# Attention and experts on one core: value tiles packed around resident ones, low parts of the keys written in place

## The chip, the cores and the metric

The kernel runs on one core of one Trainium2 chip. The metric is the device time of one execution in microseconds (us), the median of several runs; lower is better.

## The reference

Attention over q, k, v of shape (8, 8, 576, 64), in fp32, with a bias from a running sum of s, followed by a layer of 16 experts of which each token uses one:

```
scores = q @ k^T / 8 + min(-(cum[q] - cum[k]), 0),  cum = cumsum(max(s, 0)); causal
attn   = exp(scores - rowmax);  attn /= sum(attn) + 1e-9
x      = attn @ v                       -> 4608 tokens x 512
expert = argmax of a group, then argmax within it
out    = weight * relu(x @ w1[expert]) @ w2[expert]
```

The change lies in the attention part alone.

## The kernel before, in words

The 64 heads are worked off as 32 pairs p of two heads n = 2p and 2p + 1. For each pair four inputs are brought into SBUF:

- `load_raw` (L143): keys and queries of both heads, transposed, as `r` (128 partitions x 2 x 576; one head in partitions 0 to 63, the other in 64 to 127), from DRAM.
- `split` (L145 to L158): each value is cut into a rounded high part and the remainder, the low part. The high parts are cast by ScalarE (L150) into the tile `hl`, whose four slots are key high, query high, key low, query low. The low parts are a subtraction on GpSimd (L153; VectorE for pair 0): one instruction of 128 x 576 for the keys, one for the queries. `split` issues the cast, and the subtraction goes into a list "G" from which it is taken later.
- `load_a` and `load_b` (L166 to L185): DMAs within SBUF copy from `hl` into two operand tiles. `WA` gets key high and query high (64 partitions). `WB` has 128 partitions: its lower 64 hold key low and query high, its upper 64 key high and query low. For each head the lower half is one DMA (L184, 64 x 2 x 576, 288 KB) and the upper half another (L185, 288 KB). `WB` has three buffers.
- `load_v` (L187): the values, one DMA from DRAM of 480 KB. The tile `VT` holds for each of five key tiles three blocks of 64 columns: values of head 0, ones, values of head 1. The ones lie in DRAM with the values and are loaded each time. `VT` has two buffers.

TensorE then computes, for each head, row maxima (L209, `pm`, read by VectorE at L217), the scores as a product of `WA` (L265) and one of `WB` (L267) into `ps`, and the product with the values (L305, `po`). The stationary operand at L305 is 128 columns wide: values and ones side by side, so that half of `po` is the row's sum. ScalarE takes the exponential (L275) and empties `po` in two steps, `vals` (L309) and `sums` (L312). GpSimd sets what lies above the diagonal to zero (L284, AFFINE_SELECT) before L305 reads it. The shift by the row maximum goes through two small DMAs, `WA<-th` and `WA<-tl` (L243), which ScalarE issues in its own queue.

The order of work on TensorE, VectorE, ScalarE and GpSimd is written out by hand as strings of letters, one string for the step of an even head and one for that of an odd one (`ORDERS`, `FIRST`): B and C are score and value products, A row maxima, `b` an exponential, `e` a causal select, `v` the emptying of `po`, `G` a subtraction from the list, `S` a split. SyncE (SP) issues the loads; after the first steps its order is set by a scheduler from the program's order.

Of the kernel before, what the change touches and what calls it, by code (L numbers as in the profile page):

```python
# [8 lines left out]
F32 = mybir.dt.float32  # L9
# [11 lines left out]
P = 128  # L21
# [26 lines left out]
NB = 5  # L48
# [59 lines left out]
def attention(tc, qk, v, s, wr, xs, st):  # L108
# [3 lines left out]
    with ExitStack() as ctx:  # L112
# [18 lines left out]
        NA, NBB, NVT = 4, 3, 2  # L131
        WA = [wa.tile([68, 2, 2, QW], F32R, name=f"WA{i}") for i in range(NA)]
        WB = [wa.tile([P, 2, 2, S], F32R, name=f"WB{i}") for i in range(NBB)]
        VT = [big.tile([P, NB, 3, 64], F32, name=f"VT{i}", tag=f"VT{i}", bufs=1) for i in range(NVT)]
# [10 lines left out]
        def split(p, part, later=False):  # L145

            if part == 0:
                hls[p] = raw.tile([P, 4, S], F32R, name=f"hl{p}", tag="hl", bufs=3)
            hl, r = hls[p], raws[p]
            nc.scalar.copy(hl[:, part], r[:, part])  # L150

            def low():
                (nc.vector if p < 1 else nc.gpsimd).tensor_tensor(  # L153
                    out=hl[:, 2 + part], in0=r[:, part], in1=hl[:, part].bitcast(F32), op=ALU.subtract)

            if later:
                push("G", p, low)
            else:  # L158
                low()
# [16 lines left out]
        def load_b(p, placed=False):  # L176
            w = WB[p % NBB].bitcast(F32)
            hl = hls.pop(p).bitcast(F32)
            for h in range(2):

                hr = slice(h * 64, h * 64 + 64)
                a = slice(0, 1 if placed and h == 0 else 2)
                b = slice(1 if placed and h else 0, 2)
                nc.sync.dma_start(w[0:64, a, h], hl[hr, 2:0:-1][:, a])  # L184
                nc.sync.dma_start(w[64:128, b, h], hl[hr, 0::3][:, b])  # L185

        def load_v(p):  # L187
            nc.sync.dma_start(VT[p % NVT], v[p])
# [100 lines left out]
        def av(n, pt, vals, sums):  # L289
# [4 lines left out]
            for half, todo in enumerate(avs):  # L294
# [4 lines left out]
                def item(j, t, qa, qb, half=half, base=base, w=w, po=po, last=len(todo) - 1):  # L299
                    if j == 0:  # L300
# [5 lines left out]
                                     VT[p % NVT][:, t, h:h + 2].rearrange("p a d -> p (a d)"),  # L306
# [106 lines left out]
        def push(k, i, f):  # L413
            fifo[k].append((i, f))
# [67 lines left out]
        for i in range(2):  # L482
# [24 lines left out]
        ones(3)  # L507

# [1011 lines left out]
def _layout(inputs):  # L1520
# [7 lines left out]
    vv = np.ones((NP, NB * P, 3, D), dtype=v.dtype)  # L1528
    vp = v.reshape(NP, 2, S, D)
    vv[:, :S, 0], vv[:, :S, 2] = vp[:, 0], vp[:, 1]  # L1530
    vv = vv.reshape(NP, NB, P, 3, D).transpose(0, 2, 1, 3, 4)
# [30 lines left out]
```

## Time and profile before

| | us |
|---|---|
| median of 3 runs (975.96 to 977.0) | 976.94 |
| the profiled execution | 975.5 |
| its span on the core | 973.8 |

The attention takes the first 460 us or so of the span, the experts the rest. In the rows below PE is TensorE's matmul, PEld its weight load, DVE VectorE, ACT ScalarE, POOL GpSimd and SP SyncE; a trailing q (ACTq, SPq) is the engine's own queue of instructions, in which it issues DMAs. A wait is put down to the work that came last by the profile.

### The profile page before, as it was taken

How to read it: one execution, taken by the hardware profiler on the slowest of the kernel's cores; microseconds unless marked ns; L12 is line 12 of the kernel's file. 1: busy time of each engine (PE TensorE's matmuls, PEld its weight loads, DVE VectorE, ACT ScalarE, POOL GpSimd, SP SyncE). 2: the span in 40 equal slices, each digit the busy share in tenths (PEclk: the TensorE clock that was granted, in tenths of full speed). 3: DMA queues.
4: the chain of work that ended last, by engine and by line, in shares of the span. 5: the costliest groups of instructions: out<-in, count | busy, mean ns of one | idle time of the engine just before them, and what ended most of it. 6: DMA issues, size and time to landing. Idle time of an engine off the chain costs nothing. (4 is left out here: it accounts for less than half of the span.)

```text
span 973.8 us, 17866 instructions
## 1 busy us (share of the span) xinstructions
PE 881.4 (91%) x5640; PEld 790.7 (81%) x5640; DVE 747.9 (77%) x2023; ACT 610.5 (63%) x1388; POOL 550.5 (57%) x682
## 2 busy tenths in 40 slices
PE   4888998999999999998868899999999999999983
PEld 3677887887777787886657799999999999998972
DVE  7445686697868779787497679988888998888860
ACT  5556775776767667776535356676766666766640
POOL 8444455453554456443566556667776767766640
PEclk9989998999999999999888899999999999999997
DMA  7999999999999999953624444555655556655410
GB/s 201 244 221 232 244 238 217 238 240 231 233 231 229 234 222 241 228 132 113 200 85 164 172 156 154 194 196 180 216 188 183 193 180 217 217 205 205 153 42 22
DMA packets 64167, 187.25 MB, mean 192 GB/s; under 512 B 9628, under 2 KB 18460, under 8 KB 55872
## 3 DMA queue, kind: packets, MB, share of 16 engines
q1 hardware_dynamic: 54160, 166.11, 62.8%
q0 software_dynamic: 7488, 18.89, 5.5%
q10 hardware_dynamic: 2416, 1.03, 0.5%
q8 instruction: 47, 0.77, 0.3%
q14 instruction: 56, 0.46, 0.2%
HBM read 112.12 MB, written 19.69 MB: 135 GB/s over the span
## 5 line engine op out<-in xcount | busy, mean ns | idle before, releaser
L971 POOL TENSOR_TENSOR wl<-raw,wh 128x512 fp32r<-128x512 f32 x166 | 214.4, 1305 | 76.1 <-ACT wh L968 58.2
L217 DVE CUSTOM_DVE_ANT_0 mx<-pm,mask 128x192 bf16<-128x192 f32 (+4 forms) x320 | 127.7, 419 | 63.4 <-PE pm L209 61.0
L968 ACT CAST wh<-raw 128x512 fp32r<-128x512 f32 x256 | 155.1, 616 | 9.6 <-issue 9.5
L1069 PE MATMUL ph<-xl,wh 128*128 128x256 f32 (+13 forms) x512 | 146.3, 305 | 4.3 <-DVE xl L1041 4.0
L1069 PE MATMUL ph<-xh,wh 128*128 128x256 f32 (+13 forms) x512 | 145.3, 302 | 4.1 <-ACT xh L1040 4.0
L209 PE MATMUL pm<-WA 66*128 66x288 f32 (+4 forms) x384 | 126.2, 360 | 20.0 <-DMA WA<-ch 10.6
L265 PE MATMUL ps<-WA 68*128 68x320 f32 (+4 forms) x384 | 137.1, 361 | 5.8 <-ACT pu L275 2.7
L305 PE MATMUL po<-pt,VT 128*128 128x256 f32 (+3 forms) x512 | 124.5, 361 | 17.0 <-DMA VT<-in_v_dram 7.5
L284 POOL TENSOR_SCALAR_AFFINE_SELECT pt<-pt 128x128 f32<-128x128 f32 (+2 forms) x192 | 63.9, 340 | 104.9 <-ACT pt L275 102.4
L305 PEld LDWEIGHTS po<-pt,VT 128*128 128x128 f32 x512 | 88.7, 195 | 33.6 <-issue 14.2
L1124 PE MATMUL py<-hl,wh 128*128 128x256 f32 (+13 forms) x448 | 113.9, 302 | 1.7 <-DVE hl L1065 1.7
L1124 PE MATMUL py<-hh,wh 128*128 128x256 f32 (+13 forms) x448 | 113.6, 302 | 0.7 <-ACT wh L968 0.6
L267 PE MATMUL ps<-WB 128*128 128x320 f32 (+4 forms) x384 | 112.3, 305 | 0.0
L1036 DVE STREAM_TRANSPOSE xt<-xg 32x256 f32<-32x256 f32 (+1 forms) x224 | 109.5, 489 | 3.4
L1170 DVE STREAM_TRANSPOSE yr<-yT 32x384 f32<-32x384 f32 (+1 forms) x208 | 104.5, 502 | 4.3
L305 PE MATMUL po<-pu,VT 128*128 128x320 f32 (+1 forms) x384 | 106.9, 387 | 0.0
L1069 PEld LDWEIGHTS ph<-xl,wh 128*128 128x128 f32 x512 | 97.5, 190 | 7.9 <-DVE xl L1041 6.1
L1069 PEld LDWEIGHTS ph<-xh,wh 128*128 128x128 f32 x512 | 97.6, 191 | 6.1 <-ACT xh L1040 5.9
L209 PEld LDWEIGHTS pm<-WA 66*128 66x128 f32 (+1 forms) x384 | 70.3, 195 | 31.8 <-DVE mc L217 12.2
L367 POOL TENSOR_TENSOR xTl<-xT,xTh 128x512 fp32r<-128x512 f32 x30 | 38.2, 1274 | 101.8 <-ACT xTh L363 90.5
L1064 ACT ACTIVATE hh<-ph 128x256 fp32r<-128x256 f32 (+13 forms) x128 | 53.8, 420 | 62.0 <-PE ph L1069 60.9
L153 POOL TENSOR_TENSOR hl<-r,hl 128x576 fp32r<-128x576 f32 x62 | 88.0, 1422 | 4.2 <-ACT hl L150 4.2
(238 smaller groups left out, 2014.2 us busy)
## 6 DMA issues: line engine op xcount, KB each, us to landing
raw<-in_w_dram SPq DMA_DIRECT2D x64, 1024.0 KB
WB<-hl SPq DMA_DIRECT2D x122, 288.0 KB
r<-in_qk_dram SPq DMA_DIRECT2D x32, 576.0 KB
WA<-hl SPq DMA_DIRECT2D x61, 288.0 KB
VT<-in_v_dram SPq DMA_DIRECT2D x32, 480.0 KB
xs<-xr SPq DMA_DIRECT2D x15, 512.0 KB
WA<-cumd SPq DMA_DIRECT2D x56, 4.5 KB
xs<-xrt SPq DMA_DIRECT2D x7, 128.0 KB
```

The lines of the kernel that those rows point to most:

```text
L153: (nc.vector if p < 1 else nc.gpsimd).tensor_tensor(out=hl[:, 2 + part], in0=r[:, part], in1=hl[:, part].bitcast(F32), op=ALU.subtract)
L209: nc.tensor.matmul(ps[:rows, :cw], WA[i][0:66, QA, h, QO + q0:QO + q0 + rows], WA[i][0:66, KA, h, QO + c0:QO + c0 + cw], start=True, stop= ...
L217: nc.vector.tensor_tensor_reduce(out=tmp[:rows, :cw], in0=ps[:rows, :cw], in1=mk[:rows], scale=1.0, scalar=-3.0e38 if c0 == 0 else mo, op0 ...
L265: nc.tensor.matmul(ps[:rows, o:o + w], WA[i][0:68, KA, h, QO + k0:QO + k0 + rows], WA[i][0:68, QA, h, QO + q0:QO + q0 + w], start=True, st ...
L267: nc.tensor.matmul(ps[:rows, o:o + w], WB[p % NBB][:, KA, h, k0:k0 + rows], WB[p % NBB][:, QA, h, q0:q0 + w], start=False, stop=True)
L305: nc.tensor.matmul(po[0][:, qa - base:qb - base], VT[p % NVT][:, t, h:h + 2].rearrange("p a d -> p (a d)"), x[:, c:c + qb - qa], start=(j ...
L968: self.casts.append(nc.scalar.copy(h[:, j], raw[:, j]))
L971: self.low = nc.gpsimd.tensor_tensor(out=l[:, j], in0=raw[:, j], in1=h[:, j].bitcast(F32), op=ALU.subtract)
L1036: V.transpose(dst[:, 0:n, :, j], src[:, 0:n, :, i])
L1069: self.product = nc.tensor.matmul(pss[f][:, :cap], w[f // 4][:, c, (f % 4) * P:(f % 4 + 1) * P], x[:, c, :cap], start=(c == 0 and w is sel ...
L1124: self.product = nc.tensor.matmul(pss[c][:, :cap], w[2 + f // 4][:, f % 4, c * P:(c + 1) * P], x[:, f, :cap], start=(f == 0 and w is self. ...
L1170: V.transpose(dst[:, 0:n, :, i], src[:, 0:n, :, j])
```

## The change

`VT` holds per block the values of head 1 of the tile before, the values of head 0 of this tile, and ones, so that the two blocks of values lie side by side; the ones are set once, at the start, by two GpSimd MEMSETs, and the load writes only the values, in six pieces of 512 bytes per partition instead of one of 3840. The 128 columns that L305 uses are the same ones. GpSimd (VectorE for pair 0) writes the low parts of the keys straight into the lower half of `WB`, in one instruction of 64 x 576 per head, so `hl` has three slots instead of four and the DMA of the lower half of `WB` carries only the query's high part. `WB` has five buffers instead of three. The order strings get one more `G` per pair.

```diff
-        NA, NBB, NVT = 4, 3, 2
+        NA, NBB, NVT = 4, 5, 2
-        VT = [big.tile([P, NB, 3, 64], F32, name=f"VT{i}", tag=f"VT{i}", bufs=1) for i in range(NVT)]
+        VT = [big.tile([P, NB + 1, 3, 64], F32, name=f"VT{i}", tag=f"VT{i}", bufs=1) for i in range(NVT)]
...
-                hls[p] = raw.tile([P, 4, S], F32R, name=f"hl{p}", tag="hl", bufs=3)
+                hls[p] = raw.tile([P, 3, S], F32R, name=f"hl{p}", tag="hl", bufs=3)
...
-            def low():
+            def low(h):
+                hr = slice(0, P) if part else slice(h * 64, h * 64 + 64)
                 (nc.vector if p < 1 else nc.gpsimd).tensor_tensor(
-                    out=hl[:, 2 + part], in0=r[:, part], in1=hl[:, part].bitcast(F32), op=ALU.subtract)
-
-            if later:
-                push("G", p, low)
-            else:
-                low()
+                    out=hl[:, 2] if part else WB[p % NBB][0:64, KA, h], in0=r[hr, part],
+                    in1=hl[hr, part].bitcast(F32), op=ALU.subtract)
+
+            for h in range(1 if part else 2):
+                if later:
+                    push("G", p, lambda h=h: low(h))
+                else:
+                    low(h)
...
-                a = slice(0, 1 if placed and h == 0 else 2)
                 b = slice(1 if placed and h else 0, 2)
-                nc.sync.dma_start(w[0:64, a, h], hl[hr, 2:0:-1][:, a])
-                nc.sync.dma_start(w[64:128, b, h], hl[hr, 0::3][:, b])
+                if h or not placed:
+                    nc.sync.dma_start(w[0:64, QA, h], hl[hr, 1])
+                nc.sync.dma_start(w[64:128, b, h], hl[hr, 0::2][:, b])
...
-            nc.sync.dma_start(VT[p % NVT], v[p])
+            nc.sync.dma_start(VT[p % NVT][:, :, 0:2], v[p])
...
-                                     VT[p % NVT][:, t, h:h + 2].rearrange("p a d -> p (a d)"),
+                                     VT[p % NVT].rearrange("p t a d -> p (t a d)")[:, (3 * t + 1 + h) * 64:][:, 0:P],
...
+        for t in VT:
+            nc.gpsimd.memset(t[:, 0:NB, 2], 1.0)
...
-            "b S R B0 R v b a A0 B2 v C0 e G a R a B3 T C1 A3 B1 A2 C2 b e t C3 v C4 B4 J b D v e a a A1 "
+            "b S R B0 R v b a A0 B2 v C0 e G a R a B3 T C1 A3 B1 A2 C2 b e t C3 v G C4 B4 J b D v e a a A1 "
```

How the order moves. First GpSimd, around one pair in the middle of the attention; `hl`, `r`, `pt`, `pu`, `xTl` are the tiles named above, with numbers of their buffers. Before:

```order
L367 TENSOR_TENSOR xTl_768<-xT_1239,xTh_767 128x512
L284 AFFINE_SELECT pu_118<-pu_118 128x128
L284 AFFINE_SELECT pt_117<-pt_117 128x128
L153 TENSOR_TENSOR hl_1168<-r_996,hl_1168 128x576
L284 AFFINE_SELECT pt_117<-pt_117 128x2x128
L284 AFFINE_SELECT pt_117<-pt_117 64x64
L284 AFFINE_SELECT pt_115<-pt_115 128x128
L153 TENSOR_TENSOR hl_1348<-r_1165,hl_1348 128x576
L284 AFFINE_SELECT pu_116<-pu_116 128x128
L284 AFFINE_SELECT pt_115<-pt_115 128x2x128
L284 AFFINE_SELECT pt_115<-pt_115 64x64
```

and now:

```order
L371 TENSOR_TENSOR xTl_776<-xT_1250,xTh_775 128x512
L288 AFFINE_SELECT pu_120<-pu_120 128x128
L288 AFFINE_SELECT pt_119<-pt_119 128x128
L155 TENSOR_TENSOR hl_1178<-r_1005,hl_1178 128x576
L288 AFFINE_SELECT pt_119<-pt_119 128x2x128
L288 AFFINE_SELECT pt_119<-pt_119 64x64
L288 AFFINE_SELECT pt_117<-pt_117 128x128
L155 TENSOR_TENSOR WB_110<-r_1175,hl_1359 64x576
L288 AFFINE_SELECT pu_118<-pu_118 128x128
L155 TENSOR_TENSOR WB_110<-r_1175,hl_1359 64x576
L288 AFFINE_SELECT pt_117<-pt_117 128x2x128
L288 AFFINE_SELECT pt_117<-pt_117 64x64
```

The one subtraction for the keys has become two, and the second stands ahead of the last two selects of the even head's step. Next the DMAs of SP for about one pair, with what each waits for (DMAHW0 to DMAHW7 are eight semaphores that the DMAs of SP and ScalarE take in turn: a DMA that waits for DMAHW5 is issued when the last one on DMAHW5 has landed, and then uses it itself). Before:

```order
L172 DMA WA_109<-hl_2323 64x2x576 [waits DMAHW4_49,Activation_49]
L188 DMA VT_113<-in_v_dram 128x960 [waits DMAHW5_49,PE_49]
L402 DMA xs<-xr_2252 128x4x256 [waits DMAHW6_49,Activation_49]
L172 DMA WA_109<-hl_2323 64x2x576 [waits DMAHW7_49,PE_49]
L174 DMA WA_109<-cumd 2x576 [waits DMAHW0_49]
L184 DMA WB_112<-hl_2117 64x2x576 [waits DMAHW1_49,PE_49]
L185 DMA WB_112<-hl_2117 64x2x576 [waits DMAHW2_49]
L143 DMA r_2509<-in_qk_dram 128x1152 [waits DMAHW3_49,Pool_49]
L174 DMA WA_106<-cumd 2x576 [waits DMAHW6_49,PE_49]
```

and now:

```order
L192 DMA VT_115<-in_v_dram 128x6x128 [waits DMAHW3_49,PE_49]
L176 DMA WA_109<-hl_2339 64x2x576 [waits DMAHW4_49,Activation_49]
L188 DMA WB_110<-hl_2339 64x576 [waits DMAHW5_49]
L188 DMA WB_110<-hl_2339 64x576 [waits DMAHW6_49]
L406 DMA xs<-xr_2268 128x4x256 [waits DMAHW7_49,Activation_49]
L176 DMA WA_109<-hl_2339 64x2x576 [waits DMAHW0_49,PE_49]
L178 DMA WA_109<-cumd 2x576 [waits DMAHW1_49]
L144 DMA r_2526<-in_qk_dram 128x1152 [waits DMAHW2_49,Pool_49]
L189 DMA WB_110<-hl_2339 64x2x576 [waits DMAHW3_49]
L189 DMA WB_110<-hl_2339 64x2x576 [waits DMAHW4_49]
L178 DMA WA_106<-cumd 2x576 [waits DMAHW7_49,PE_49]
```

The value load now stands ahead of the loads of `WA` and `WB`, and the loads of `WB` no longer wait for TensorE. The gap in the numbers before the last row is ScalarE's two small DMAs, which stand in its queue ahead of `sums`. Before:

```order
L309 COPY vals_2413<-po_0_2540 64x256 [waits PE_49]
L275 ACTIVATE pt_115<-ps_2_0_2555 128x512 [waits Pool_49]
L243 DMA WA_107<-th_2574 1x10x128 [waits DMAHW4_49,DVE_49]
L243 DMA WA_107<-tl_2575 1x10x128 [waits DMAHW5_49,DVE_49]
L312 ACTIVATE sums_2414<-po_0_2540 64x256
```

and now:

```order
L313 COPY vals_2430<-po_0_2557 64x256 [waits PE_49]
L279 ACTIVATE pt_117<-ps_2_0_2572 128x512 [waits Pool_49]
L247 DMA WA_107<-th_2591 1x10x128 [waits DMAHW5_49,DVE_49]
L247 DMA WA_107<-tl_2592 1x10x128 [waits DMAHW6_49,DVE_49]
L316 ACTIVATE sums_2431<-po_0_2557 64x256
```

Read with SP's rows: before, they are issued when a load of `WA` (on DMAHW4) and one of `VT` (on DMAHW5) have landed; now, when two loads of `WB` of half the former size have (on DMAHW5 and DMAHW6).

## Rows read from the trace of the kernel before

**Rows 1.** The page: busy time of each engine, and DMA busy tenths in 40 slices.
```profile
PE 881.4 (91%) x5640; PEld 790.7 (81%) x5640; DVE 747.9 (77%) x2023; ACT 610.5 (63%) x1388; POOL 550.5 (57%) x682
DMA  7999999999999999953624444555655556655410
```

**Rows 2.** Busy time by stage; the last three columns: granted clock, DMA share, GB/s.
```profile
25.00:56.00 31.00, 26.28 (x120) 22.16 (x120) 11.96 (x50) 15.41 (x36) 12.66 (x21) 0.89 1.04 240
56.00:167.82 111.82, 101.11 (x596) 86.30 (x595) 73.10 (x272) 77.28 (x192) 54.71 (x93) 0.94 1.01 230
167.82:400.63 232.81, 219.86 (x1389) 182.50 (x1388) 183.95 (x654) 163.09 (x410) 120.67 (x200) 1.00 1.00 233
400.00:425.00 25.00, 24.97 (x164) 22.11 (x163) 21.11 (x83) 18.14 (x46) 12.68 (x24) 1.00 0.88 213
```

**Rows 3.** What TensorE waits for, 60 to 430 us: total, times, longest.
```profile
PE po L305 <- DMA VT<-in_v_dram: 7.5, 5, 2.5
PE pm L209 <- DVE mc L217: 5.7, 7, 1.9
PE po L305 <- DMA WA<-tl: 4.3, 4, 1.4
PE po L305 <- ACT sums L312: 2.3, 1, 2.3
PE ps L265 <- DMA WA<-tl: 0.8, 2, 0.7
```

**Rows 4.** One such wait: TensorE's row at 278.56 us.
```profile
278.56 0.67 PE L305 MATMUL po<-pt,VT 128*128 128x256 f32 x2 [1.33 <-DMA WA<-tl]
```

**Rows 5.** ScalarE's rows just before it: start, duration, in brackets idle before.
```profile
275.75 0.72 ACTq L243 DMA_DIRECT2D WA<-th  x1
277.29 0.75 ACTq L243 DMA_DIRECT2D WA<-tl  x1
278.08 0.38 ACT L312 ACTIVATE sums<-po 64x256 f32<-64x256 f32 x1 [2.29 <-DVE mc L217]
```

**Rows 6.** DMA issues of the page: count, and size of one.
```profile
WB<-hl SPq DMA_DIRECT2D x122, 288.0 KB
VT<-in_v_dram SPq DMA_DIRECT2D x32, 480.0 KB
WB<-hl SPq DMA_DIRECT2D x6, 144.0 KB
```

**Rows 7.** Stretches with a lower granted clock (columns as in rows 2).
```profile
48.00:53.00 5.00, 4.68 (x17) 4.27 (x18) 1.46 (x8) 2.43 (x7) 2.55 (x5) 0.50 1.04 226
92.00:96.00 4.00, 4.00 (x22) 3.84 (x20) 2.27 (x10) 3.66 (x10) 2.62 (x4) 0.66 1.00 207
156.00:160.00 4.00, 2.36 (x7) 2.08 (x8) 0.50 (x5) 1.36 (x4) 0.23 (x1) 0.52 0.94 190
160.00:164.00 4.00, 4.00 (x20) 3.84 (x20) 2.26 (x8) 3.46 (x9) 2.58 (x4) 0.63 0.92 199
```

**Rows 8.** DMA queues of the page: packets, MB, share of 16 engines over the span.
```profile
q1 hardware_dynamic: 54160, 166.11, 62.8%
q10 hardware_dynamic: 2416, 1.03, 0.5%
```

**Rows 9.** L153: duration in ns (least, median, most), first and last start.
```profile
L153 POOL TENSOR_TENSOR hl<-r,hl x62: 1397/1408/1972, 11.8 to 409.2; 128x576 fp32r<-128x576 f32 x62
```

**Rows 10.** ScalarE, 167 to 401 us: the same columns on 128 and on 64 partitions.
```profile
L275 ACT ACTIVATE pt<-ps 128x256 f32<-128x256 f32 x34 | 13.0, 382 | 0.1
L312 ACT ACTIVATE sums<-po 64x256 f32<-64x256 f32 x34 | 12.8, 378 | 34.5 <-DVE mc L217 20.9 <-DVE xT L350 8.7 <-DVE st L342 4.7
```

**Rows 11.** GpSimd in an even step, then TensorE's reader of that block.
```profile
262.55 0.28 POOL L284 TENSOR_SCALAR_AFFINE_SELECT pu<-pu 128x128 f32<-128x128 f32 x1
262.80 0.40 POOL L284 TENSOR_SCALAR_AFFINE_SELECT pt<-pt 128x256 f32<-128x256 f32 x1
268.35 0.70 PE L305 MATMUL po<-pt,VT 128*128 128x320 f32 x2
```

**Rows 12.** GpSimd at the start: a MEMSET of 576 columns.
```profile
3.31 0.59 POOL L474 MEMSET mask<- 128x576 f32 x1
```

**Rows 13.** VectorE's product of two SBUF tiles (least, median, most, ns).
```profile
L350 DVE TENSOR_TENSOR xT<-vals,st x27: 758/759/1559, 74.1 to 426.2; 128x576 f32<-128x576 f32 x27
```

More of the change, by code (lines that the diff above doesn't have):

```diff
@@ L1526, in _layout @@
     qk = np.stack([k.transpose(0, 1, 3, 2).reshape(NP, P, S), q.transpose(0, 1, 3, 2).reshape(NP, P, S)], axis=2)
[L1528 to L1531, printed above, removed]
+    vp = np.zeros((NP, 2, NB * P, D), dtype=v.dtype)
+    vp[:, :, :S] = v.reshape(NP, 2, S, D)
+    vp = vp.reshape(NP, 2, NB, P, D).transpose(0, 3, 2, 1, 4)
+    vv = np.zeros((NP, P, NB + 1, 2, D), dtype=v.dtype)
+    vv[:, :, 1:, 0], vv[:, :, :NB, 1] = vp[:, :, :, 1], vp[:, :, :, 0]
     return {
```

4 rows, old and new, of the table FIRST are left out of this document.

## The prediction

> **What bounds the kernel now.** I read the engines' totals first, then the stages of the attention, then the waits of the busiest engine there, and last the queue that those waits lead to. TensorE is busy for 91% of the span, and the DMA engines are at nine tenths or more in every slice from 24 to about 415 us [rows 1]. By stage [rows 2] the DMA share is 1.04, 1.01 and 1.00 from 25 to 400.63 us, at 230 to 240 GB/s: the transfers fill that time completely. TensorE is busy for 26.28 + 101.11 + 219.86 = 347.25 of the same 375.63 us. So two resources are close to their limits, and TensorE still idles for 28 us (some of which are matmuls missing from the records). The fourth row of that group shows the same kind of work once the last pairs need no more loads: the DMA share falls to 0.88, and TensorE is busy for 24.97 of 25.00 us.
>
> What are the idle times? Between 60 and 430 us TensorE waits 7.5 us for loads of the values, 4.3 + 0.8 us under the name of the small DMA WA<-tl, 2.3 us for ScalarE's `sums`, and 5.7 us for VectorE [rows 3]. The name WA<-tl needs a second look. At 278.56 us the value product had waited 1.33 us [rows 4]. In ScalarE's queue [rows 5] the DMA `th` was issued at 275.75, `tl` only at 277.29, and `sums`, which stands behind them and empties the PSUM tile that the product needs, ran from 278.08 to 278.46. TensorE started 0.10 us later. ScalarE was held up while issuing a DMA of 5 KB: by the order shown above, `tl` is issued only when the value load eight DMAs earlier has landed, and that one is late because the DMA engines are full. So I count the first, third, fourth and fifth row of [rows 3] as one cause, full DMA engines: 7.5 + 4.3 + 2.3 + 0.8 = 14.9 us.
>
> **What the change takes from the DMA engines.** Before, `WB` costs 122 x 288 + 6 x 144 = 36000 KB and the values 32 x 480 = 15360 KB [rows 6]. After it, the 29 pairs with full loads need 2 x 144 + 2 x 288 = 864 KB of `WB` each, the first three 576 KB: 26784 KB. The values need 128 x 768 x 4 bytes = 384 KB a pair, 12288 KB. The cut is 9216 + 3072 = 12288 KB, or 12.6 MB. At the 233 GB/s of the long stage [rows 2] that is 54 us of transfer time out of 376, 14%. The DMA engines would be done in 86% of the time in which they are now at their limit. That is the share at which the fourth row of [rows 2] shows no idle TensorE; so DMA stops setting the pace, and TensorE's own work does. The gain is therefore not 54 us but what TensorE now waits for.
>
> The pieces of the values get smaller: 768 of 512 bytes instead of 128 of 3840. No row shows a load from DRAM in such pieces. From below, ScalarE's queue moved 2416 packets of 426 bytes on average in 0.5% of 16 engines x 973.8 us, so 32 ns each; from above, SP's queue took 181 ns for a packet of 3.1 KB [rows 8]. At 32 ns a load takes 768 x 32 / 16 = 1.5 us of all engines, at 181 ns 8.7 us; before, 480 KB at 233 GB/s took 2.1. I take 35 ns, which is 512 bytes at 233/16 GB/s, since the packets of 426 bytes are nearest in size, and keep the other end for a rival.
>
> **The sum**, on the profiled execution of 975.5 us (span 973.8; 1.4 below the median of the runs).
>
> - Waits for DMA, direct and through ScalarE: minus 14.9 us. Bounds: nothing, and all of the 15.
> - Clock. Four stretches ran at a mean granted clock of 0.50, 0.66, 0.52 and 0.63 [rows 7], that is partly at 1.2 instead of 2.4 GHz; the third begins with TensorE idle (2.36 us busy of 4.00). Time at half clock in them: 5.0 + 2.7 + 3.8 + 3.0 = 14.5 us, of which half, 7, is lost where TensorE is the bound. I take minus 5, because the first stretch lies in the start, which keeps other idle times; bounds 0 and minus 7.
> - Start, 25 to 56 us. TensorE is idle for 4.7 of 31 us and DMA is at 1.04 [rows 2]. Minus 2, bounds 0 and minus 4.7.
> - GpSimd at the start: two more subtractions ahead of the first select, for pairs 1 and 2, 2 x 1.41 us [rows 9], and two MEMSETs of 320 columns, 0.59 x 320/576 = 0.33 each [rows 12], together 3.5 us. They stand in GpSimd's queue ahead of the first selects, but GpSimd is busy for only 12.66 of the 31 us that follow [rows 2], so that part of it is made up. Plus 2, bounds 0 and 3.5.
> - The extra subtraction per pair. A form of 64 partitions does not occur at L153. On ScalarE 64 partitions take as long as 128 (378 and 382 ns [rows 10]), so I take the full 1.41 us; bounds 0.7 (by partitions) and 2.8. Times 31 it is 44 us on GpSimd, which is busy for 120.67 of 232.81 us in the long stage [rows 2] and stays below 65%. Cost zero: in its new place it delays two selects by 1.41 us, of which the first would end at 263.20 us, while TensorE reads that block at 268.35 [rows 11]: 5.1 us of cover. If that is gone, C2 of the value product is late next.
> - Waits dropped from the loads of `WB` (five buffers instead of three): SP issues them earlier. Nothing is behind that but the value load, which now stands ahead of them; zero.
> - The 5.7 us for VectorE stay. The experts' part keeps its instructions; a few at the seam change places: zero, within 3 us either way.
>
> Sum: 975.5 - 14.9 - 5 - 2 + 2 = 955.6, say **956 us**.
>
> **A rule against the change.** VectorE's product of two SBUF tiles takes 0.76 us at the median and up to 1.56 [rows 13]; so something now and then costs it 0.8 us. The Trainium skill, "GPSIMD Engine Reference", section "1. Specifications", says that GpSimd's SBUF interfaces are shared with VectorE, and names instructions with two SBUF inputs as contending. By that rule the new 44 us of subtractions would slow such instructions; without it they cost nothing. It is the third rival.
>
> **The rivals.**
>
> 1. *The wait only changes its name.* DMA stays the pace for part of the time: the engines are still needed for 86% of it, the loads come in bursts, and ScalarE still issues `th` and `tl` ahead of `sums`, 0.72 and 0.75 us each [rows 5]. For it speaks that the issue itself fills much of ScalarE's 2.29 us there. Against it speaks the stretch from 400 us on. With half of the DMA term and half of the clock: 975.5 - 7.5 - 2.5 = 965.5.
> 2. *Small pieces cost more than their bytes* (the other side). The cut in `WB` saves 9216 KB, 40 us of transfer, 1.27 us a pair. The value load has 2.1 us a pair now; it eats the saving when 768 x t / 16 = 3.4 us, at t = 70 ns per piece, between the two ends above. Past that the DMA engines are the bound, harder than now. At t = 100 ns a load takes 4.8 us, 1.4 more than the break-even, over 29 pairs plus 41 us: 1017. For it speaks that the bound of 181 ns is not excluded; against it the 32 ns of the smaller packets.
> 3. *VectorE is slowed by GpSimd.* If each of the 31 new subtractions costs VectorE 0.8 us, it gets 25 us more work in a stage in which it is busy for 79% (183.95 of 232.81 [rows 2]), so it is no bound; but the row maxima come later, and the 5.7 us that TensorE waits for them may double: 961.5. The median of [rows 13] is the least value too, which speaks against much of it.
> 4. *No change:* TensorE's idle times come from the hand-written order, and the full DMA engines only get a name that belongs to others. Then the sum is 975.5 plus 0 to 2. Against it stands the chain of [rows 4, 5].
>
> **How the numbers follow.** Forecast (945 to 961): 0.56; rival 1: 0.20; rival 3: 0.10; rival 4: 0.06; rival 2: 0.08. Two runs of this kernel can be told apart at about 0.2%, 2 us. Forecast and rivals 1 and 3 are faster by more: 0.86. Rival 4 splits into 0.05 the same and 0.01 slower; with rival 2 slower is 0.09. With all lower bounds the sum is 975.5 - 14.9 - 7 - 4.7 = 949, less 3 for the seam and some of the VectorE term 943; upwards the range takes in rivals 1 and 3, with 3.5 at the start and 3 at the seam, to 970.
>
> **What would show it.** Right, if the stage up to about 380 us has a DMA share near 0.9, if TensorE's waits for the value load and for WA<-tl fall to a few us, and if ScalarE's wait ahead of `sums` (34.5 us [rows 10]) shrinks to little more than the two issues. GpSimd's L155 should show 31 instructions more at 1.4 us. Wrong, if the DMA share stays at 1.0 with fewer GB/s (rival 2), if the waits for VectorE grow (rival 3), or if selects appear as what TensorE waits for.

## The result

The changed kernel takes 968.51 us (median of 20 runs, 962.0 to 979.11), the kernel before 976.97 us in the same comparison (20 runs, 970.19 to 984.03). The ratio is 0.9909, with a 95% interval of 0.9884 to 0.9934: about 0.9% faster, and 12.5 us above the 956 forecast. The profiled execution of the change took 967.23 us, its span is 965.5 us; the sum of the prediction was made against 975.5 and 973.8 us. A single execution of either kernel varies by some 0.4% around its median, so every comparison below stands on medians and intervals, and the traces are read for places and mechanisms.

The page of the changed kernel: busy time of the engines, and DMA busy tenths in 40 slices (compare [rows 1]).

```profile
PE 879.6 (91%) x5640; PEld 791.4 (82%) x5640; DVE 755.9 (78%) x2024; ACT 609.3 (63%) x1388; POOL 597.3 (62%) x715
DMA  6999989898989889622634445465555555655410
```

Busy time by stage in the first three stretches of [rows 2], changed kernel; the columns are those of that group, the last three granted clock, DMA share and GB/s.

```profile
25.00:56.00 31.00, 26.39 (x127) 21.71 (x127) 14.51 (x64) 16.20 (x39) 17.98 (x28) 1.00 0.96 221
56.00:167.82 111.82, 105.14 (x623) 89.64 (x622) 80.33 (x283) 79.31 (x199) 71.19 (x104) 0.94 0.95 217
167.82:400.63 232.81, 221.18 (x1405) 186.27 (x1404) 191.64 (x665) 165.41 (x416) 146.32 (x218) 0.99 0.85 203
```

The DMA share in the long stage fell from 1.00 to 0.85, as forecast, and GpSimd has 25.65 us more to do there. But TensorE does hardly more work in these 232.81 us: 221.18 in place of 219.86. VectorE, to which the change gives no work there, went from 183.95 to 191.64 us, with 11 instructions more in the window. What TensorE waits for, 60 to 430 us, changed kernel (compare [rows 3]):

```profile
PE pm L213 <- DVE mc L221: 14.1, 11, 2.0
PE po L309 <- ACT sums L316: 3.5, 1, 3.5
PE po L309 <- issue: 0.4, 1, 0.4
```

Of the 14.9 us that the prediction put down to full DMA engines, 3.5 are left, in one piece near 63 us; the loads of the values and WA<-tl are gone from the list. (The length of the piece near 63 us changes from execution to execution: e6 and e11 below are the same kernel and show 4.3 and 2.0 us.) The wait for VectorE's row maxima has gone up from 5.7 to 14.1 us.

**Where the lead is won.** The transposes of the row maxima (L231 before, L235 now) mark each pair's place. First the changed kernel, then two marks of the kernel before; two more marks of that kernel, 167.82 and 400.63 us, are the bounds of its long stage in [rows 2].

```profile
52.66 0.27 PE L235 MATMUL pmt<-ident,mc 128*10 128x128 f32 x1
74.21 0.27 PE L235 MATMUL pmt<-ident,mc 128*10 128x128 f32 x1
...
162.08 0.27 PE L235 MATMUL pmt<-ident,mc 128*10 128x128 f32 x1
...
392.41 0.27 PE L235 MATMUL pmt<-ident,mc 128*10 128x128 f32 x1
```

```profile
55.99 0.27 PE L231 MATMUL pmt<-ident,mc 128*10 128x128 f32 x1
71.43 0.27 PE L231 MATMUL pmt<-ident,mc 128*10 128x128 f32 x1
```

The change leads by 3.3 us at the first mark, is 2.8 behind at the second, leads by 5.7 at the third and by 8.2 at the last. The execution ends 8.3 us earlier: the experts' part neither won nor lost. The long stage between the third and the fourth mark gave only 232.81 - 230.33 = 2.5 us. A kernel's long stage is compared below by the same two marks, since it repeats better than the start: e6 and e11, one and the same kernel, take 222.7 and 222.4 us for it, while their second marks stand at 74.70 and 70.78 us.

**What holds VectorE.** TensorE's new stalls come at regular distances: 1.31 or 1.32 us at 192.91, 246.21, 299.50 and 354.42, and 1.51 or 1.52 us at 216.12, 269.41, 322.69 and 377.87 us, one of each kind per batch of four pairs. Here is one of the first kind in the changed kernel: first GpSimd, then VectorE, then TensorE, each row with its start and its duration.

```profile
241.45 1.42 POOL L155 TENSOR_TENSOR WB<-r,hl 64x576 fp32r<-64x576 f32 x1
242.82 0.35 POOL L288 TENSOR_SCALAR_AFFINE_SELECT pu<-pu 128x128 f32<-128x128 f32 x1
243.25 1.40 POOL L155 TENSOR_TENSOR WB<-r,hl 64x576 fp32r<-64x576 f32 x1
```

```profile
243.32 1.37 DVE L827 TENSOR_TENSOR u<-pos,thr 128x25 f32<-128x25 f32 x1
244.73 0.17 DVE L830 TENSOR_REDUCE us<-u 128x5 f32<-128x20 f32 x1
...
245.67 0.47 DVE L221 CUSTOM_DVE_ANT_0 mx<-pm,mask 128x320 bf16<-128x320 f32 x1
```

```profile
244.67 0.22 PE L271 MATMUL ps<-WB 128*64 128x64 f32 x1
246.21 0.75 PE L213 MATMUL pm<-WA 66*64 66x64 f32 x2 [1.31 <-DVE mc L221]
```

The router's subtraction `u<-pos,thr` has 25 columns, yet it takes 1.37 us. It starts 0.07 us after GpSimd's second subtraction (the one that the change adds) and ends at 244.69, 0.04 us after GpSimd does. The row maximum behind it, `mx` at 245.67, runs late; it frees the PSUM tile that TensorE's next product of queries and keys needs. The stall of 1.51 us has the same form: at 266.55 us a cast of 128x5 takes 1.37 us while GpSimd, in the first of the two subtractions, works from 266.48 to 267.90. In the kernel before, another cast of the same shape was caught in the same way by the one subtraction for the keys; TensorE waited 1.94 us then, and as long once more at 386.09. Kernel before, GpSimd, VectorE and TensorE:

```profile
219.07 1.40 POOL L153 TENSOR_TENSOR hl<-r,hl 128x576 fp32r<-128x576 f32 x1
219.18 1.32 DVE L884 CAST c<-rem 128x5 bf16<-128x5 f32 x1
221.60 0.36 PE L209 MATMUL pm<-WA 66*128 66x192 f32 x1 [1.94 <-DVE mc L217]
```

By their mean duration, 56 to 430 us, before and after:

```profile
L821 DVE TENSOR_TENSOR u<-pos,thr 128x25 f32<-128x25 f32 x6 | 1.1, 186 | 0.2
L882 DVE CAST c<-cw 128x5 bf16<-128x5 f32 x5 | 1.1, 223 | 0.1
```

```profile
L888 DVE CAST c<-cw 128x5 bf16<-128x5 f32 x6 | 5.9, 979 | 0.2
L827 DVE TENSOR_TENSOR u<-pos,thr 128x25 f32<-128x25 f32 x6 | 5.9, 978 | 0.2
```

Not every operation of VectorE is caught. The row maxima, which read PSUM, the transposes, the reciprocals and the reductions have the same durations beside a subtraction as without one. Held were sums, products and differences of two SBUF tiles, casts from SBUF to SBUF, and the sum of an SBUF tile and a constant.

### The profile page after: what moved, and what is told of

The parts are those of the page before. It is cut to its first block, busy times and chain, and to the rows that moved or that the text cites. A ratio compares the mean times of both kernels' runs of the same rounds, so it can differ in the third digit from the quotient of the medians.

```text
span 965.5 us, 17856 instructions
## 1 busy us (share of the span) xinstructions
PE 879.6 (91%) x5640; PEld 791.4 (82%) x5640; DVE 755.9 (78%) x2024; ACT 609.3 (63%) x1388; POOL 597.3 (62%) x715
## 3 DMA queue, kind: packets, MB, share of 16 engines
q1 hardware_dynamic: 70496, 153.52, 57.2%
## 5 line engine op out<-in xcount | busy, mean ns | idle before, releaser
L309 PE MATMUL po<-pu,VT 128*128 128x320 f32 (+1 forms) x384 | 109.3, 393 | 0.0
L155 POOL TENSOR_TENSOR WB<-r,hl 64x576 fp32r<-64x576 f32 x62 | 87.5, 1411 | 5.6 <-ACT hl L151 3.1
```

The source lines that it names most:

```text
L155: (nc.vector if p < 1 else nc.gpsimd).tensor_tensor(out=hl[:, 2] if part else WB[p % NBB][0:64, KA, h], in0=r[hr, part], in1=hl[hr, part]. ...
L309: nc.tensor.matmul(po[0][:, qa - base:qb - base], VT[p % NVT].rearrange("p t a d -> p (t a d)")[:, (3 * t + 1 + h) * 64:][:, 0:P], x[:, c: ...
```

## The experiments

Theory 1: a GpSimd subtraction holds VectorE's operations on SBUF until it ends, and TensorE then waits for the row maxima. Theory 2: VectorE was late before too, and the waits for DMA only hid it. Theory 3: the place of the subtractions matters for another reason than what VectorE meets there. Each kernel's ratio is to the kernel before, timed beside it; "long stage" is the time between the two marks, in one execution; "wait for mc" is TensorE's, 60 to 430 us; "u" is the mean of `u<-pos,thr`, 56 to 430 us.

| kernel | median us | ratio (95% interval) | long stage, us | wait for mc, us | u, ns |
|---|---|---|---|---|---|
| before | 976.97 | 1 | 232.8 | 5.7 | 186 |
| changed | 968.51 | 0.9909 (0.9884 to 0.9934) | 230.3 | 14.1 | 978 |
| e1, one key subtraction a pair | 965.97 | 0.9865 (0.982 to 0.9911) | 226.3 | 9.8 | 188 |
| e2, both moved | 959.6 | 0.9815 (0.9767 to 0.9864) | 221.3 | 1.8 | 186 |
| e3, keys' part alone | 967.82 | 0.9929 (0.9896 to 0.9962) | 229.2 | 14.1 | 976 |
| e4, values' part alone | 980.16 | 0.999 (0.995 to 1.0029) | | | |
| e5, before with its subtraction moved | 977.57 | 1.001 (0.9976 to 1.0043) | 235.5 | 0.6 | 186 |
| e6, e3 with both moved | 958.13 | 0.981 (0.9762 to 0.9858) | 222.7 | 3.4 | 186 |
| e7, e2 and two more subtractions | 980.35 | 1.0032 (1.0003 to 1.0061) | 233.8 | 14.8 | 875 |
| e8, e2 and two pairs of selects | 964.15 | 0.9867 (0.9823 to 0.991) | 229.7 | 10.0 | 379 |
| e13, changed, each subtraction halved | 964.24 | 0.9851 (0.9817 to 0.9886) | 223.8 | 7.7 | 328 |

### e1: without the second key subtraction

In `split` of the changed kernel:

```
-            for h in range(1 if part else 2):
+            for h in range(1 if part or p >= NBB else 2):
```

> The changed kernel without the second key subtraction on GpSimd for the pairs from 5 on: the low part of the second head's keys is left as an older pair wrote it, so a sixteenth of the scores' low terms is computed from old data. Time without it is what the added subtractions cost. Theory 1 (in the trace of the changed kernel a GpSimd subtraction holds VectorE's small operations on SBUF, 128x25 at 1374 ns in place of 186 ns, and TensorE then waits for the row maxima): the stall of 1.31 us in each batch of four pairs goes, the stall of 1.51 us under the first subtraction stays; some ten stalls less, 6 to 13 us, so 955 to 962 us, and u<-pos,thr is back near 190 ns. Theory 2 (VectorE was late before too and the waits for DMA only hid it): the mean of u<-pos,thr falls, but TensorE's wait for mc stays near 14 us in 60 to 430 us, and the time within 2 us of the changed kernel's.

Measured: 965.97 us. The stalls of 1.31 us are gone, `u<-pos,thr` is back at 188 ns, and the four stalls of 1.51 or 1.52 us under the first subtraction stand at 219.99, 272.11, 326.36 and 378.64 us. That is theory 1 to the place. The wait for mc is 9.8 in place of 14.1 us, so theory 2, by which it would have stayed, does not hold for the added subtraction. But 9.8 is still 4.1 more than the 5.7 of [rows 3], with no more subtractions for the keys than in the kernel before: for that part theory 2 is right, since holds under the old subtraction now show in full. The time gained less than the 6 us that was the least expected: 2.5 us by the medians, and the two intervals overlap. The long stage is 4.0 us shorter; at the start this execution lost more, with 5.4 us of waiting for `sums` near 66 us in place of 3.5.

### e2: both subtractions moved

```
-  "... v C0 e G a R a B3 T ... v G C4 B4 J b D v e a a A1 ...",
-  "C0 B2 A4 ...
+  "... v C0 e a R a B3 T ... v C4 B4 J b D v e G a a A1 ...",
+  "C0 G B2 A4 ...
```

> The changed kernel with both GpSimd subtractions of the keys moved in the order of the work: the first behind the third select of the even head, the second behind the first select of the odd head, where VectorE reduces PSUM and transposes. Theory 1: the operations that were held under the subtractions are short again, the stalls of 1.31 and 1.51 us per batch shrink to under 0.5 us each, TensorE's wait for mc in 60 to 430 us falls from 14.1 us to under 6, and the time to 953 to 960 us. If other work of VectorE is held in the new places instead, new operations of over 1.3 us stand there and the time stays within 3 us of the changed kernel's. Theory 2: the stalls stay at their places and the time does not move.

Measured: 959.6 us, ratio 0.9815; its interval ends at 0.9864, below the 0.9884 at which that of the changed kernel begins. The edit moves work and leaves none out. TensorE's waits, 60 to 430 us, e2:

```profile
PE po L309 <- ACT sums L316: 3.0, 1, 3.0
PE po L309 <- issue: 2.5, 5, 0.9
PE ps L269 <- DMA WA<-tl: 2.4, 4, 1.0
PE pm L213 <- DVE mc L221: 1.8, 3, 1.1
```

The wait for mc fell from 14.1 to 1.8 us. The stretch from 182 to 392 us, first in the changed kernel, then in e2 (columns as in the table by stage above):

```profile
182.00:392.00 210.00, 198.44 (x1261) 167.68 (x1260) 173.97 (x601) 149.99 (x378) 134.02 (x200) 0.99 0.86 207
```

```profile
182.00:392.00 210.00, 206.52 (x1316) 172.32 (x1314) 175.80 (x631) 157.71 (x394) 140.87 (x208) 1.00 0.95 214
```

TensorE is busy for 206.52 of 210 us; with pairs coming faster the DMA share rises to 0.95. From mark to mark (162.73 to 384.06 us) the stage takes 221.3 us, 9.0 less than in the changed kernel: the whole difference of the two medians, 8.9 us. The hold itself has not gone. It falls on the product `xT<-vals,st`, whose mean rises from 850 to 1234 ns, and TensorE waits for VectorE for only the 1.8 us above:

```profile
L354 DVE TENSOR_TENSOR xT<-vals,st 128x576 f32<-128x576 f32 x29 | 35.8, 1234 | 1.0
...
L888 DVE CAST c<-cw 128x5 bf16<-128x5 f32 x6 | 1.4, 240 | 0.2
L827 DVE TENSOR_TENSOR u<-pos,thr 128x25 f32<-128x25 f32 x6 | 1.1, 186 | 0.2
```

### e3 and e4: each half of the change alone

e3 is the changed kernel with the values as they were; e4 is the kernel before with the values packed. In e3:

```
-        VT = [big.tile([P, NB + 1, 3, 64], ...
+        VT = [big.tile([P, NB, 3, 64], ...
-            nc.sync.dma_start(VT[p % NVT][:, :, 0:2], v[p])
+            nc.sync.dma_start(VT[p % NVT], v[p])
...
```

> The changed kernel with the values left as they were before (480 KB a pair, the ones loaded from memory): only the keys' part of the change. It takes 9.2 of the 12.3 MB off the DMA queue and has both GpSimd subtractions. Theory 1: VectorE's stalls as in the changed kernel (1.31 and 1.51 us per batch); a part of the waits for VT is back, 2 to 5 us: 969 to 974 us. Theory 2: as many waits of TensorE in sum, but VectorE's small operations need not explain them.

> The kernel before with the values packed and the ones set once by GpSimd: 3.1 of the 12.3 MB off the queue, 96 KB and some 0.4 us of every pair, and one subtraction per pair as before. Theory 1: no new VectorE stall, so each us of DMA wait that goes is kept: TensorE's waits that end at a transfer fall from 14.9 us by 4 to 10, mc's stay at 5 to 7 us; 967 to 973 us. Theory 2: what goes of the DMA's waits comes back as waits for VectorE: mc's rise to 8 us or more, and the time stays over 972 us.

Measured: 967.82 and 980.16 us. The keys' part alone is as good as the whole change (0.9929 and 0.9909, with intervals that overlap), with the same stalls at the same distances; the waits for value loads that theory 1 expected are not there. The values' part alone shows no gain (0.999; the interval allows 0.5%), where theory 1 had expected 967 to 973 us. Theory 2's "over 972" came true, but which waits of TensorE stand behind it is left open, so its sign, a longer wait for mc, can't be judged. The keys' part holds three things: fewer bytes, the loads of `WB` that no longer wait for TensorE (five buffers), and the value load earlier in SP's order. No run takes them apart; that the bytes are what counts is argued from the DMA share of 1.00.

### e5: the kernel before with its subtraction moved

```
-  "... v C0 e G a R a B3 T ...",
-  "C0 B2 A4 ...
+  "... v C0 e a R a B3 T ...",
+  "C0 G B2 A4 ...
```

> The kernel before with nothing but its GpSimd subtraction of the keys moved from the first select of the even head to the first select of the odd head. Theory 1 (a subtraction on GpSimd holds VectorE, and this only shows where no transfer is late): in the kernel before three stalls of TensorE for mc, 0.8 to 1.95 us, 4.7 us in sum, are of this kind; they go, but the queue sets the pace there, so that at most half of it is kept: 973 to 977 us. Rival theory 3 (the new order is better by itself, whatever the change): it gains here what it gained on the changed kernel, some 9 us: 966 to 970 us.

Measured: 977.57 us, ratio 1.001 (0.9976 to 1.0043). The move that gave 9 us on the changed kernel gives nothing here, and theory 3 falls in the form that the new order is better whatever the change. TensorE's waits, 60 to 430 us, e5:

```profile
PE po L305 <- DMA VT<-in_v_dram: 14.0, 8, 2.8
PE po L305 <- DMA WA<-tl: 8.3, 6, 2.0
PE ps L265 <- DMA WA<-tl: 4.1, 5, 1.3
...
PE pm L209 <- DVE mc L217: 0.6, 2, 0.4
```

The wait for VectorE fell from 5.7 to 0.6 us, and the waits for transfers rose from the 12.6 us of [rows 3] to 26.4. While the queue sets the pace, taking off VectorE's stalls only makes TensorE wait longer for transfers. So theory 2 has a part of the truth: in the kernel before, VectorE's holds and the late transfers covered each other. Taking off the holds alone won nothing; taking off the late transfers alone won a part and brought out holds that were there before, as e1 shows.

### e6: the keys' part alone, with both subtractions moved

e3 with the order of e2.

> The moved order with the keys' part alone: the values as they were before, 480 KB a pair. With VectorE's stalls gone the DMA engines were busy 0.91 to 1.03 of the time from 100 to 380 us, so that 96 KB more per pair, at some 220 GB/s 0.4 us of each pair, should show as waits for VT or for WA<-tl: 962 to 967 us, TensorE's waits for transfers in 60 to 430 us 5 us or more. If the packed values are worth nothing, it stands within 2 us of the moved order with them, 958 to 962 us.

Measured: 958.13 us here and 957.76 when run again (e11, below), beside 959.6 for e2: without the packed values it is as fast, within intervals of 0.5%, and TensorE waits for no value load from 60 to 430 us. SP's queue over 56 to 430 us (packets, MB, share of 16 engines): first e6, with 480 KB a load, then e2, with 384 KB.

```profile
q1 hardware_dynamic: 35823, 77.56, 86.8%
```

```profile
q1 hardware_dynamic: 54563, 74.30, 88.3%
```

e2 moves 3.3 MB less in 18740 packets more, and its queue is busy no less. By these two rows the value load in 512-byte pieces takes as much of the queue's time as the longer one did.

### e7 and e8: two subtractions more, or four selects

Both start from e2 and put work back at the two places from which the subtractions were moved. A select here reads one tile and writes one; the results go to a tile that nobody reads.

```
+  "... v C0 e H a R a B3 T ... v H C4 B4 J b D v e G a a A1 ...",
...
+  # e7
+  nc.gpsimd.tensor_tensor(out=scr, in0=mask[0:64], in1=mask[0:64], op=ALU.subtract)
...
+  # e8
+  for _ in range(2):
+      nc.gpsimd.affine_select(out=scr, in_=mask[0:64], pattern=[[1, S]], ...)
```

> The moved order with one more GpSimd subtraction (64x576, two inputs from SBUF, into a tile that nobody reads) at each of the two places from which the keys' subtractions were moved. Theory 1: the held operations are back (u<-pos,thr and the 128x5 cast near 1.37 us), TensorE's stalls of 1.3 and 1.5 us per batch are back, its waits for mc in 60 to 430 us are 8 to 15 us, the time 966 to 971 us. Theory 3 (what mattered was when the keys' low parts are ready, not what VectorE meets): the time stays at 957 to 962 us.

> As the kernel with the extra subtractions, but at each of the two places GpSimd runs two selects of 64x576 (one input each), about as long in sum, into a tile that nobody reads. Theory 1, in the form that the hold belongs to operations with two inputs from SBUF: u<-pos,thr and the cast stay under 0.5 us, no stall comes back, 957 to 963 us. If any work of GpSimd holds VectorE, or if the load on GpSimd is what costs, it is as slow as with the extra subtractions, 966 to 971 us.

Measured: 980.35 and 964.15 us. VectorE's held operations, 56 to 430 us, first e7, then e8:

```profile
L834 DVE TENSOR_TENSOR u<-pos,thr 128x25 f32<-128x25 f32 x6 | 5.3, 875 | 0.2
L828 DVE TENSOR_TENSOR off<-off,hot 128x80 f32<-128x80 f32 x6 | 4.8, 798 | 0.0
```

```profile
L836 DVE TENSOR_TENSOR u<-pos,thr 128x25 f32<-128x25 f32 x6 | 2.3, 379 | 0.2
```

With the subtractions back in those places the hold is back (875 ns, the wait for mc 14.8 us in 13 pieces); the cast of 128x5 was not caught this time (202 ns), other casts and differences were. Theory 3, by which only the time at which the keys' low parts are ready counts, falls here. The loss, 20 us against e2, is larger than theory 1 priced. The profiled execution of e7, 971.7 us, is the fastest of its twelve and shows 10 us more than e2 at the pair that e2 reaches at 384.06 us. Part of it is TensorE's clock: behind stalls of 1.95 to 1.97 us for mc at 214.16, 269.10 and 324.05 us the granted clock was 0.50 to 0.54 (216 to 218, 270 to 272 and 324 to 326 us), while in the changed kernel, with stalls of 1.51 us there, it fell once. The other eleven executions have no trace, but their mean granted clocks are 0.956 to 0.962, against 0.968 in this one; 0.009 of 978 us would be the 9 us between it and the median, by estimate.

The selects cost 4.6 us by the medians (intervals overlap) and 8.4 us of the long stage; the median lies between the two expectations, and the form of theory 1 tied to two inputs of the GpSimd instruction does not stand: `u<-pos,thr` takes up to 0.60 us there. A select of this size took 660 ns on average, a subtraction 1202 ns in e7; four selects keep GpSimd busy for no less than two subtractions, 44.9 and 40.9 us from 167 to 401 us. That pointed to the length of one instruction, and to e13.

### e13: the changed kernel, each subtraction in two halves

```
-                (nc.vector if p < 1 else nc.gpsimd).tensor_tensor(
-                    out=... WB[p % NBB][0:64, KA, h], in0=r[hr, part], ...)
+                for c in (slice(0, S // 2), slice(S // 2, S)):
+                    (nc.vector if p < 1 else nc.gpsimd).tensor_tensor(
+                        out=... WB[p % NBB][0:64, KA, h, c], in0=r[hr, part, c], ...)
```

> The changed kernel, order and places as they are, with each GpSimd subtraction cut into two of 288 columns. If VectorE is held for as long as one instruction of GpSimd lasts: the held operations (u<-pos,thr and the 128x5 cast, 1.37 us) fall to 0.8 us or less, TensorE's stalls of 1.3 and 1.5 us per batch to some 0.7 us each, its waits for mc in 60 to 430 us from 14.1 to 5 to 9 us, the time to 960 to 965 us. If what counts is how long GpSimd works in sum, nothing falls and it stays at 966 to 971 us.

Measured: 964.24 us, `u<-pos,thr` 328 ns, the wait for mc 7.7 us: these three are inside their expected ranges. The interval of the ratio, 0.9817 to 0.9886, just touches that of the changed kernel; the long stage, 223.8 us, is 6.5 us shorter. The first kind of stall fell from 1.31 to some 0.37 us, the second only from 1.51 to between 0.97 and 1.27, where 0.7 was expected: in the rows below two operations in a row are held, one by each half. VectorE and TensorE in e13:

```profile
261.71 0.74 DVE L891 CAST c<-rem 128x5 bf16<-128x5 f32 x1
262.48 0.68 DVE L892 TENSOR_TENSOR c<-rem,c 128x5 bf16<-128x5 f32 x1
263.59 0.36 PE L214 MATMUL pm<-WA 66*128 66x192 f32 x1 [1.01 <-DVE mc L222]
```

Of VectorE's operations on up to 100 columns none lasts longer than 0.80 us from 56 to 430 us; a half takes 0.79 at the median. GpSimd does the same work in the same places, and only the length of one instruction changed. So one operation of VectorE is held for as long as the instruction that it meets, not by the load on GpSimd.

### e9 to e12 and e14: the start

Near 63 us the changed kernel and the seven others above with the keys in place lose 1.7 to 5.4 us of TensorE's time. ScalarE's rows there, changed kernel, and then TensorE's:

```profile
56.57 0.60 ACT L279 ACTIVATE pt<-ps 128x512 f32<-128x512 f32 x1
61.29 0.75 ACTq L247 DMA_DIRECT2D WA<-th  x1
62.44 0.73 ACTq L247 DMA_DIRECT2D WA<-tl  x1
63.21 0.38 ACT L316 ACTIVATE sums<-po 64x256 f32<-64x256 f32 x1 [6.04 <-DMA WA<-th]
```

```profile
63.69 0.77 PE L309 MATMUL po<-pt,VT 128*128 128x256 f32 x1 [3.47 <-ACT sums L316]
```

It is the pattern of [rows 5], with a longer wait. e9 puts the sums ahead of the issue in the kernel of e6 (`D v e G` becomes `v D e G` in the even heads), e10 sends th and tl on SyncE's queue (`nc.scalar.dma_start` becomes `nc.sync.dma_start` in `send`), e11 and e12 are e6 and e9 once more on one chip, e14 is e9's edit on the changed kernel.

> The moved order with the keys' part alone, and in the even heads ScalarE copies the sums before it issues the transfers of th and tl (it issued them first). In every kernel with the keys in place TensorE loses 3 to 4.6 us near 63 us, because the sums stand behind the issue of th, which itself waits for a transfer of the backlog at the start. If that is the loss at the start, the stall near 63 us falls under 1.5 us and the time by 2 to 4 us, to 954 to 957 us; if the next step on ScalarE or TensorE waits in its place, it stays within 1.5 us of the kernel without it, 957 to 960 us.

> The moved order with the keys' part alone, and th and tl are sent on SyncE's queue in place of ScalarE's. If ScalarE's waiting to issue th is all that is lost at the start, it is as good as with the sums first, 954 to 957 us. If th then waits behind the loads of later pairs on SyncE, TensorE waits for WA<-tl by more than 1 us in many pairs and the time goes over 962 us.

> The moved order with the keys' part alone once more, to stand beside the kernel with the sums first on one chip. If the stall near 63 us is what the sums' place is worth, it is 2 to 5 us slower than that kernel; else within 1.5 us of it.

> The kernel with the sums first once more, beside the one that differs from it by that alone. If the stall near 63 us is what the sums' place is worth: 2 to 5 us faster, some 954 us; else within 1.5 us.

> The changed kernel with only the sums copied before th and tl are sent in the even heads; the subtractions stay where they are. If the stall near 63 us and VectorE's stalls are two separate losses, this one gives its 3 us here too: 964 to 966 us, with the stalls of 1.31 and 1.51 us per batch unchanged and TensorE's wait of 3.5 us near 63 us gone. If they are one, it stays within 1.5 us of the changed kernel.

Measured: e9 954.81, e10 955.07, e11 957.76, e12 954.69, e14 968.67 us. The wait for `sums` is gone in e9, e12 and e14, but waits for transfers take its place: in e14 1.8 us for the value load at 61.84, in e12 0.9 us at 60.46 and 4.5 us for WA<-tl at three later places. Side by side (e11 and e12) the sums first are 3.1 us better by the medians; between e6 and e9, which were not timed together, the medians differ by 3.3 us but the ratios are 0.981 and 0.9818. On the changed kernel they are worth nothing (968.67 and 968.51). The ratios of e11 and e12, 0.982 (0.9781 to 0.986) and 0.978 (0.9746 to 0.9814), overlap, and their profiled executions reach the last pair's mark together, at 415.57 and 415.60 us; the long stage takes 222.4 and 222.1 us. Whether there is a gain of 3 us is not settled. What the traces do show is that the start stays bound by transfers: in the changed kernel the DMA share is still 1.00 from 60 to 72 us.

The lowest median is e12's, which has the keys in place, the values unpacked, the subtractions moved and the sums first: 954.69 us, ratio 0.978, against 968.51 of the change. e2, e6, e9 and e10 stand within 5 us of it, with intervals that overlap.

## Why the prediction was right and wrong

- **What bounded the kernel**: right. The full DMA engines were the bound. The waits for value loads and WA<-tl have gone from the long stage, the share is 0.85 (0.9 was the sign asked for), and e5 shows from the other side that a faster VectorE did not help as long as the queue was full. One row does not carry what was read from it: the DMA share of 0.88 at 400 to 425 us [rows 2] is a mean over a share of 0.95 to 1.05 from 405 to 416 us and lower ones around it, and TensorE was busy for all of those 11 us too. So it does not show that a share of 0.86 frees TensorE; the 206.52 of 210 us in e2 at 0.95 do. The sign from ScalarE was badly chosen: its idle time ahead of `sums` did not shrink (34.9 us against the 34.5 of [rows 10]), though the late transfers went, so it was no measure of them.
- **The bytes**: right, 166.11 [rows 8] to 153.52 MB, 12.6 less. But "the cut is 9216 + 3072" KB counts two unlike halves. The keys' part brought the whole gain (e3), the values' none that shows (e4, and e2 beside e6). The 35 ns for a 512-byte piece were too low: if 768 of them occupy the queue as long as the old load's 2.1 us, as e2 beside e6 says, one takes 2.1 x 16 / 768 = 44 ns, an estimate, still near the lower bound and below the 70 ns at which rival 2 would have come. That the five buffers of `WB` are worth nothing, as the prediction has it, was not tested.
- **The sum's term of 14.9 us**: 11.4 of it went, by the rows. What is left is the 3.5 us at the start, where the prediction's sentence "DMA stops setting the pace" does not hold.
- **"The 5.7 us for VectorE stay"**: this is the step that failed. They became 14.1 us, 8.4 more. e1 (the added subtraction left out), e2 (both moved, wait 1.8 us, 8.9 us faster), e7 (put back) and e13 (halved) show that GpSimd's subtractions are the cause. By e1, 4.3 of the 8.4 us go with the added subtraction. The other 4.1 are left without it, in stalls under the old one (four of 1.51 or 1.52 us) that showed only in part while transfers were late.
- **"The extra subtraction per pair: cost zero"** is half of the same failure, seen from GpSimd's side. Its price of 1.41 us was right (64 partitions take 1404 ns at the median, 128 took 1408), and the two selects behind it were covered, as worked out: from 60 us on no wait of TensorE ends at a select. The cover was looked for only among those who read GpSimd's results, and not among the operations of VectorE that run beside it.
- **Rival 3** had the mechanism and the place, doubled waits for mc, at a chance of 0.10 and a time of 961.5 (955.6 + 5.7 is 961.3). Its sign, "if the waits for VectorE grow", is the one that came. It counted the new subtractions alone. It was set aside because the median of VectorE's large product was undisturbed [rows 13]. That row shows a wide operation that seldom meets a subtraction; the small ones of the router, which in the old order already met subtractions, were not looked at. Rival 1 named a time nearer to the measured one, 965.5, but that is luck: by it the waits for transfers would have stayed in half, and of its mechanism only the start is seen. The Trainium skill has the rule in a sharper form than the line that the prediction cited: "SBUF — State Buffer", section "🔬 SBUF: two separate sides", calls the shared pair of ports an exclusive lock that the first comer keeps for its whole instruction while the other waits. The traces agree: an operation of 0.19 us took 1.37 us and ended 0.04 us after GpSimd's of 1.40; with halves of 0.79 us no small operation lasted longer than 0.80, and the reductions and operations on PSUM were left alone.
- **The clock, minus 5**: mis-sized. By the granted clocks of [rows 2] 31 x 0.11 + 111.82 x 0.06 = 10.1 us were lost; now 111.82 x 0.06 + 232.81 x 0.01 = 9.0. [rows 7] leaves out another stretch, 64 to 68 us at 0.58. All but the first stand behind waits of TensorE of 2.1 to 2.5 us, two for value loads and one for `sums`; before the first, from 44 to 48 us, it was busy for 1.59 of 4 us. Those waits went, but the changed kernel has four such stretches too: 56.5 to 60 us at 0.53, behind a wait of 1.9 us for ScalarE; 64 to 70 us at 0.50, behind the stall at 63 us; 138 to 142 and 323 to 327 us, both at 0.58, behind waits of 2.01 and 1.51 us for mc. So stalls that the change left or brought out have cost clock as well. About 1 us in place of 5.
- **Start, minus 2, and GpSimd there, plus 2**: the sum of nothing was close (25 to 56 us: TensorE busy 26.39, was 26.28), for other reasons. GpSimd's extra work shows as one wait of TensorE for a select, 0.7 us at 44.45, and the change leads by 3.3 us at the first mark. The loss of 6.1 us between the first two marks holds the stall of 3.5 us and the low clock behind it; that a backlog of transfers is the cause is argued from the share of 1.00 there.
- **The seam and the experts, zero**: right, 8.2 us of lead at the last pairs, 8.3 at the end.

Put together: 955.6 + 8.4 (VectorE) + 3.5 (DMA waits left) + 4 (clock) = 971.5, against 967.2 measured. The list is 4 us too long; which of its pieces overlap is not shown. With the subtractions moved out of the way (e2) the change stands at 959.6, inside the forecast's own range of 945 to 961: what was missed is the one mechanism, and not the value of relieving the queue. The prediction's 0.2% for telling two runs apart was too small: with 6 to 20 runs the intervals here are 0.25% to 0.5% wide on each side.

## What to carry to other kernels

Work that is given to an engine with time to spare still has neighbours: before pricing a GpSimd instruction at nothing, list which VectorE operations between SBUF tiles will be waiting to start beside it, in the order of the program, and who waits for what stands behind them. If it must run there, place it where VectorE works from PSUM or transposes, or cut it up, since one hold lasts as long as one instruction; but operations that follow each other can then be held one after the other. And when two waits cover each other, as the queue and VectorE did here, expect the second to come out when the first is removed, and price it from the rows of both.

## What was not expected of the hardware

- An operation of VectorE on 128x25 or 128x5 elements took 1.37 us in place of 0.17 to 0.19 while GpSimd subtracted two SBUF tiles, and up to 0.65 us beside selects of 64x576 that read one. The casts of 5 columns were held as the differences were; transposes, reductions, reciprocals and reads of PSUM were not.
- GpSimd's subtraction of 576 columns takes the same 1.40 us on 64 partitions as on 128.
- With value loads from DRAM in 512-byte pieces and a fifth fewer bytes (384 in place of 480 KB), SP's queue was occupied no less than with pieces of 3840 bytes: 88.3% with 74.30 MB beside 86.8% with 77.56 MB.
